# The hand-written order of the opening: the same steps in other places on the compute engines' queues

## The chip, the cores and the metric

One core of a Trainium2 chip. The metric is the device time of the kernel in microseconds, the median of several runs. One execution was also taken by the profiler; all times of single instructions come from that execution and are counted from the start of its span.

## The reference

A gated linear attention recurrence, whose output goes through a feed-forward block with a hard-swish gate. Everything is float32 (the weights come in as float64, as pairs of 32-bit words).

```python
# q, k, v, alpha: (batch 4, heads 8, seq 768, head_dim 48)
for t in range(S):
    state = alpha[:, :, t, :, None] * state + np.einsum('bhd,bhe->bhde', k[:, :, t], v[:, :, t])
    y[:, :, t] = np.einsum('bhd,bhde->bhe', q[:, :, t], state)
x = y.transpose(0, 2, 1, 3).reshape(B * S, H * D)       # 3072 x 384
h = x @ w_in                                            # 384 x 2048
g = h * np.clip(h + 3.0, 0.0, 6.0) / 6.0
out = g @ w_out                                         # 2048 x 384
```

## The kernel before

**Chunks and groups.** The 4 x 768 tokens are 24 chunks of 128 tokens (index `j`), six for each batch element. Two chunks make a group `g` of 256 tokens, for which the feed-forward block is computed. Groups 0 and 1 (chunks 0 to 3) take a plain path; from group 2 on, both matrix products go through sums and differences of blocks, with fewer multiplications (steps `M`, `n`, `o`, `e`, `h`; the second product does so from group 1 on, steps `s`, `P`, `K`, `G`). For that, sums of weight blocks have to be made first (`y` for `w_in`, `x` for `w_out`).

**The order.** Nothing is scheduled by the compiler. A string of words is run from first to last, and each word calls one step, which issues its instructions on one engine's queue. Each engine takes its own queue strictly in that order, and an instruction waits for its operands and buffers by semaphores. So the string sets five queues at once, and nothing else does. A word is a step's name and its numbers: `sc.1.0.2` is `scores(1, 0, 2)`.

**The steps of the opening**, by engine (line numbers are those of the profile):

- SP, loads: `la`, `lk`, `lq` (alpha, k, q of a chunk, L251; from chunk 6 on in blocks, L262), `lv` (v of a chunk in two halves, L272), `w.i` (one of 16 weight slices, L162, L166). A slice lands in one of five raw buffers, and a later slice reuses it.
- A weight slice is then made into float32 by `d1` (ACT, L186), `d2` (ACT, L196), `dx` (ACT, L191, slices 0, 1, 2, 4 only), `d3` (DVE, two instructions L203, L205 for those slices, three L207, L208, L210 for the others) and `d4` (POOL, L217), which needs all the others.
- Attention: `ta`, `tk`, `tq` transpose a chunk of alpha, k, q on PE (L282; from chunk 6 on DVE, L286). `ca` copies alpha (ACT, L300); `r` and `p` are scans over it (DVE, L309 and L320, `r` with a small reciprocal L313); `k` and `q` scale the transposed k and q (DVE, L332). `kb` transposes k back (PE, L374), `ck` copies it (ACT, L378). `u` is the state's update (PE, L429), `sm.j.0` and `sm.j.1` add it to the state (DVE, L437, L439), `st` decays the state (POOL, L409). `sc` computes scores (PE, L346), `m` masks them (DVE, L356, four instructions). `sv` and `qa` (ACT, L419, L366) put the state and q beside v and the scores; `sv.0.0` is a memset on POOL (L415). `ya`, `yb` give the chunk's output (PE, L455), `cy` copies it to `xT` (ACT, L464).
- Feed-forward of groups 0 and 1: `fa.i`, `fb.i` (PE, L489: one block of the first product for chunk 0, then for chunk 1), `f.g.i.m` (PE, L478: the same for a whole group), `fr` (ACT, L494) and `fg` (DVE, L498) the gate; `b` (PE, L516) the second product of group 0.
- `z` are idle matmuls on the identity (PE, L532).

**Buffers that order steps.** PSUM has four banks for the attention, `banks[0..3]`, and four for the feed-forward, `bank_m[0..3]`; the last numbers of a word say which it uses (`kb.2.0`: bank 0; `sc.2.0.2`: banks 0 and 2; `f.1.0.2`: block pair 0 of group 1, in `bank_m[2]`). A step that writes a bank waits until the step that reads its former contents is through. So `u.1.3.1` writes banks 3 and 1, `sm.1.0` reads bank 3, and `ya.0.3` can then write it.

**The padding.** From chunk 6 on, chunks are loaded in blocks into the tiles `quads`, two sets of three. The 16 columns that a load leaves unwritten must hold ones. Before, `load_akq` set them itself on POOL (`nc.gpsimd.memset`, L257, 32 partitions x 64 elements, two per tile) with the first load into each tile, ahead of that load's DMAs.

Of the kernel before, what the change touches and what calls it, by code (L numbers as in the profile page):

```python
# [17 lines left out]
def kernel(  # L18
# [228 lines left out]

    def load_akq(name, j):
        src = rows({"a": alpha, "k": k, "q": q}[name], j)
        if j < FIRST:  # L250
            nc.sync.dma_start(out=ring[name, j % NR][:, :, 0:D],  # L251
                              in_=src.rearrange("h s d -> s h d"))
            return
        to = quads[name, j % NQ]
        if j < FIRST + NQ:
            for o in (BLK, 3 * BLK):
                nc.gpsimd.memset(to[o : o + BLK, :, V - 1, D - BLK : BLK], 1.0)  # L257
        to = to.rearrange("r p v d -> r p (v d)")
        t = src.rearrange("(p a) (u v) d -> a u p (v d)", a=2, v=V)
        for o in range(4):  # L260
            skip = BLK * (o % 2)
            nc.sync.dma_start(out=to[BLK * o : BLK * (o + 1), :, 0 : V * D - skip],  # L262
                              in_=t[o // 2, :, :, skip : V * D])
# [457 lines left out]
    def store2(g, i):  # L721
# [8 lines left out]
        "lq": lambda j: load_akq("q", j), "lv": load_v, "w": load_weight,  # L730
# [14 lines left out]
    def run(words):  # L745
        for word in words.split():
            name, *at = word.split(".")
            steps[name](*(int(x) for x in at))

    with tc.manual_schedule():  # L750
        run("""z.0.5 z.0.3 z.0.1 z.0.8 qa.0.0 w.0 d2.0 d3.0 la.0 ta.0.0 ca.0 r.0 lk.0 tk.0.1 k.0
               z.0.2 p.0 la.1 ta.1.2 lq.0 tq.0.3 ca.1 r.1 lk.1 lv.0.0 sv.0.0 d1.0 kb.0.0 ck.0 z.0.2
               u.0.2.1 sm.0.0 sv.0.1 q.0 qa.0.1 tk.1.0 k.1 p.1 z.0.2 sc.0.2.3 m.0 la.2 ta.2.0 ca.2
               dx.0 w.2 d2.2 kb.1.0 ck.1 lq.1 r.2 sm.0.1 st.1 tq.1.2 q.1 d3.2 z.0.3 d1.2 dx.2 lv.1.1
               u.1.3.1 sv.1.0 sm.1.0 p.2 sm.1.1 sc.1.0.2 m.1 ya.0.3 yb.0 cy.0 lq.2 w.1 d1.1 tq.2.1
               q.2 d4.2 lk.2 tk.2.3 k.2 fa.2.0 d4.0 st.2 sc.2.0.2 d2.1 d3.1 m.2 dx.1 d4.1 qa.1.1
               lk.3 la.3 ta.3.1 ca.3 la.4 fa.0.1 sv.1.1 w.3 r.3 ta.4.3 ca.4 r.4 tk.3.1 k.3 kb.2.0
               qa.1.0 d2.3 ya.1.2 yb.1 cy.1 fa.1.2 lq.3 ck.2 d1.3 p.3 d3.3 lv.2.2 u.2.3.2 sm.2.0
               d4.3 fb.2 tq.3.1 q.3 fb.1 qa.2.0 sm.2.1 sv.2.0 st.3 fr.0.2.0 fg.0.2 lk.4 tk.4.0
               sv.2.1 w.5 d2.5 k.4 d3.5 d1.5 qa.3.0 d4.5 qa.2.1 sc.3.1.3 m.3 w.6 d2.6 d1.6 d3.6 d4.6  # L760
               lv.3.0 lq.4 w.7 kb.3.2 fb.0 f.0.3.3 kb.4.0 ya.2.1 ck.3 u.3.3.2 sm.3.0 fr.0.3.1 fg.0.3
               fr.0.1.0 fg.0.1 qa.3.1 sv.3.0 sm.3.1 p.4 d2.7 sv.3.1 d1.7 d3.7 d4.7 f.0.5.0 fr.0.5.1
               fr.0.0.0 fg.0.5 fg.0.0 tq.4.3 ck.4 la.5 ta.5.2 f.0.6.3 ca.5 w.4 d2.4 ya.3.0 yb.3 cy.3
               fr.0.6.1 yb.2 cy.2 w.9 d2.9 q.4 qa.4.1 d1.4 d1.9 dx.4 la.6 w.8 d3.4 r.5 lk.5 w.10
               d3.9 p.5 ca.6 fg.0.6 d4.9 w.12 lq.5 lv.4.1 d2.8 d3.8 f.0.7.2 d1.8 st.4 d4.8 d4.4 w.11
               fr.0.7.0 fg.0.7 f.1.7.0 fr.1.7.1 fg.1.7 sc.4.0.2 m.4 f.1.1.1 fr.1.1.0 fg.1.1 f.1.3.3
               fr.1.3.1 d2.10 d1.10 tk.5.3 f.1.0.2 d2.12 d3.10 d4.10 w.13 fg.1.3 fr.1.0.0 fg.1.0 k.5
               d3.12 lq.6 f.1.6.0 f.1.2.1 u.4.1.0 sm.4.0 d1.12 d4.12 sv.4.0 qa.4.0 ya.4.2 fr.1.6.1
               fg.1.6 w.15 tq.5.3 fa.4.3 sv.4.1 d2.11 kb.5.1 d2.13 fr.1.2.0 f.1.4.2 fr.1.4.1 d1.11
               sm.4.1 q.5 r.6 d3.11 d3.13 fg.1.4 d4.11 lv.5.0 lk.6 tq.6 p.6 d2.15 d3.15 fg.1.2 d1.13  # L770
               d4.13 sc.5.0.3 yb.4 f.1.5.0 fr.1.5.1 fg.1.5 tk.6 m.5 b.1.0.2 fb.4 b.1.1 d1.15 d4.15
               st.5 y.5 w.14 la.7 lk.7 cy.4 d2.14 qa.5.1 ck.5 b.0.0.1 fr.0.4.0 d3.14 k.6 q.6 ca.7
               fg.0.4 d1.14 d4.14 x.0 y.1 y.10 b.0.1 y.0 y.2 u.5.2 P.1.0.0 K.1.0 qa.5.0 sv.5.0
               qa.6.1 P.1.1.3 b.0.2 b.1.2 kb.6.0 ya.5.3 y.6 s.1.0.0 sm.5.0 sv.5.1 G.1.0.0 tk.7
               s.1.1.1 s.1.2.3 x.1 yb.5 cy.5 b.1.3 sc.6.1.2 lv.6.2 ck.6 u.6.3.0 s.1.3.2 x.2 P.1.2
               b.0.3 K.1.1 y.7 s.1.4 s.1.5 y.11 y.3 r.7 xc.2.1 x.3 y.4 y.8 xc.2.3 k.7 xc.2.0 xc.2.4
               y.9 y.12 y.16 y.13 y.15 P.1.3.3 K.1.2 P.1.4 bo.1 P.1.5 xc.2.5 G.1.1.1 P.1.6 y.14 y.17
               y.19 xc.2.6 sm.6.0 G.1.2.2 y.20 M.2.0.2 lv.12.1 la.8 O.1.1 O.1.0 ca.8 y.18 y.21 y.23
               so.1 G.1.3.3 n.2.0.8 bo.0 lq.7 lv.7.0 O.1.2 m.6 xc.2.2 xc.2.10 xc.2.7 tq.7 r.8 p.7
               xc.2.8 sv.6.1 M.2.15.3 M.2.1 kb.7.3 n.2.1.9 M.2.16 M.2.2 n.2.2.10 M.2.7.0 n.2.7.11  # L780
               sm.6.1 xc.2.9 q.7 p.8 M.2.3 M.2.4 n.2.4.12 M.2.8 o.2.0.0 M.2.5 n.2.5.13 qa.7.0 sv.6.0
               st.7 lk.8 O.1.3 lq.8 lk.9 la.9 la.10 tk.8 tq.8 lq.10 lq.9 ya.6.1 yb.6 M.2.9 z.1.3
               M.2.18.1 o.2.1.0 e.2.1.1 M.2.10 cy.6 ck.7 sc.7.0.2 u.7.1.3 n.2.10.14 M.2.11 qa.7.1
               ca.9 la.11 y.22 M.2.6.2 h.2.1 q.8 m.7 e.2.0.0 h.2.0 n.2.11.15 qa.6.0 n.2.18.10 qa.8.1
               M.2.12 M.2.19 n.2.12.12 M.2.13 sm.7.0 sv.7.1 r.9 k.8 o.2.3.0 sv.7.0 ya.7.0 y.24
               o.2.5.0 n.2.13.12 o.2.2.0 yb.7 cy.7 sc.8.1.2 xc.3.1 o.2.2.1 e.2.2.1 xc.3.3 o.2.3.1
               M.2.14 xc.3.4 xc.3.0 xc.3.5 o.2.4.0 xc.3.7 xc.3.6 o.2.6.0 P.2.0.1 M.3.0.2 M.2.17
               h.2.2 o.2.6.1 e.2.3.0 h.2.3 o.2.7.0 K.2.0 n.3.0.12 M.3.1 n.3.1.9 e.2.5.1 M.3.7.0
               n.3.7.13 xc.3.8 o.2.7.1 xc.3.2 kt.8 e.2.6.0 h.2.6 tk.9 M.3.2 n.3.2.10 e.2.4.0 P.2.1.3
               h.2.4 h.2.5 s.2.0.14 e.2.7.0 G.2.0.1 h.2.7 M.3.3 M.3.4 n.3.4.8 k.9 s.2.1.11 M.3.8  # L790
               o.3.0.0 ca.10 kt.9 P.2.3.3 s.2.2.15 s.2.3.14 lv.8.2 kw.8 kr.8 lk.10 sm.7.1 xc.3.9
               M.3.5 n.3.5.11 K.2.2 e.3.0.1 xc.3.10 M.3.9 o.3.1.0 P.2.2 K.2.1 u.8.0.3 M.3.18.2 s.2.5
               M.3.10 n.3.10.14 n.3.18.15 e.3.1.0 s.2.4 P.2.4 tq.9 h.3.0 st.8 sv.8.0 M.3.11 n.3.11.8
               tk.10 p.9 sm.8.0 q.9 r.10 k.10 qa.9.0 qa.9.1 m.8 sm.8.1 h.3.1 M.3.19 o.3.5.0 kt.10
               P.2.5 G.2.2.0 st.9 M.3.12 sc.9.0.1 qa.8.0 n.3.12.10 o.3.3.0 kw.9 lv.9.0 kr.9 sv.8.1
# [137 lines left out]
```

## Time and profile before

| | |
|---|---|
| median of 3 runs | 534.24 us (534.19 to 534.98) |
| profiled execution, its own time | 533.84 us |
| its span, first to last instruction | 531.80 us |
| PE busy | 522.2 us (98%) |
| PE weight loads busy | 496.9 us (93%) |
| DVE busy | 477.0 us (90%) |
| ACT busy | 257.4 us (48%) |
| POOL busy | 50.4 us (9%) |
| HBM read, written | 44.50 MB, 8.91 MB |
| granted TensorE clock, mean | 1.0 |

A row of the timeline has the start in us, the duration in us, engine, line, operation, output and inputs, shapes and the number of instructions merged; in brackets the idle time of the engine before it and what ended it. Busy times of PE run to the modelled end of a matmul, which is later than the start of the next one. PEld is the loading of weights into PE, which runs beside the matmuls.

### The profile page before, as it was taken

To read this page: it belongs to the slowest core of one execution; us is meant where nothing else is said; L and a number is where in the kernel's file an instruction comes from. 1 tells how busy PE (TensorE), PEld (TensorE's weight loads), DVE (VectorE), ACT (ScalarE), POOL (GpSimd) and SP (SyncE) were. 2 spreads that over 40 slices of the span, in tenths; PEclk is the share of its full clock that TensorE was granted. 3 is DMA by queue.
4 is the path that set the end of the run, shared out by engine and by line. 5 is a ranking of instruction groups with operands and counts; after the bars stand their busy time and mean duration, and the time that the engine had idled before them with its cause. 6 is when DMAs were issued, how large, how long until landed. Compare 5 with 4: busy or idle time off the path is not lost.

```text
span 531.8 us, 15143 instructions
## 1 busy us (share of the span) xinstructions
PE 522.2 (98%) x6306; PEld 496.9 (93%) x6306; DVE 477.0 (90%) x849; ACT 257.4 (48%) x503; POOL 50.4 (9%) x71
## 2 busy tenths in 40 slices
PE   7799999999999999999999999999999999999997
PEld 7698886789999999999999999999999999999997
DVE  6999989999999999999999999999999899496382
ACT  3889865212653553553544444642634544553340
POOL 5333425100000000000000000000000000000000
PEclk9999999999999999999999999999999999999999
DMA  9998887006615156254345356055364052100001
GB/s 173 218 254 247 211 231 156 18 2 149 155 31 118 30 125 139 49 137 100 89 107 118 90 123 143 18 134 111 92 138 105 10 110 44 44 2 2 15 16 37
DMA packets 124100, 54.40 MB, mean 102 GB/s; under 512 B 83328, under 2 KB 116864, under 8 KB 124032
## 3 DMA queue, kind: packets, MB, share of 16 engines
q1 hardware_dynamic: 124032, 53.44, 44.0%
q8 instruction: 49, 0.80, 0.7%
q14 instruction: 19, 0.16, 0.1%
HBM read 44.50 MB, written 8.91 MB: 100 GB/s over the span
## 4 chain that ended last, share of the span: by engine, by line
PE 81%; DVE 9%; ACT 3%; DMA 3%; POOL 2%; issue 1%; SPq 0%; DVEq 0%; POOLq 0%; ACTq 0%
PE m_ps L703 34%; PE m_ps L600 34%; PE m_ps L478 4%; PE t_ps L455 3%; PE t_ps L346 2%; PE t_ps L429 2%; DMA v<-in_v_dram 1%; DMA raw<-in_moe_w_out_dram 1%; DVE rings L647 1%; DVE R L309 1%; DVE raw L537 1%; ACT raw L186 1%; DVE g_sb L647 1%; ACT raw L191 1%; DVE w L537 1%
## 5 line engine op out<-in xcount | busy, mean ns | idle before, releaser
L606 ACT COPY g_sb<-m_ps 128x512 f32<-128x512 f32 x110 | 63.6, 584 | 123.7 <-PE m_ps L600 104.3
L703 PE MATMUL m_ps<-w,g_sb 128*128 128x192 f32 x704 | 121.7, 327 | 0.0
L703 PEld LDWEIGHTS m_ps<-w,g_sb 128*128 128x128 f32 x704 | 113.7, 190 | 0.4
L703 PE MATMUL m_ps<-rings,g_sb 128*128 128x192 f32 x528 | 91.5, 326 | 0.0
L703 PEld LDWEIGHTS m_ps<-rings,g_sb 128*128 128x128 f32 x528 | 85.4, 190 | 0.1
L600 PE MATMUL m_ps<-xc,w 128*128 128x128 f32 x640 | 82.8, 277 | 0.4 <-DVE w L541 0.4
L600 PEld LDWEIGHTS m_ps<-xc,w 128*128 128x128 f32 x640 | 77.5, 192 | 1.7 <-issue 0.6
L494 ACT ACTIVATE r<-g_sb,half 128x512 f32<-128x512 f32 x80 | 56.8, 722 | 33.1 <-DVE g_sb L541 12.1
L498 DVE SCALAR_TENSOR_TENSOR g_sb<-r,g_sb 128x512 f32<-128x512 f32 x80 | 53.7, 683 | 4.3 <-ACT r L494 3.9
L600 PE MATMUL m_ps<-xT,raw 128*128 128x128 f32 x400 | 52.5, 277 | 0.0
L600 PEld LDWEIGHTS m_ps<-xT,raw 128*128 128x128 f32 x400 | 48.6, 192 | 0.6
L409 POOL TENSOR_TENSOR st<-sm,R 128x192 f32<-128x192 f32 x20 | 12.9, 643 | 352.2 <-DVE sm L439 305.5
L647 DVE TENSOR_TENSOR g_sb<-g_sb 128x512 f32<-128x512 f32 (+1 forms) x55 | 41.9, 792 | 0.2
L600 PE MATMUL m_ps<-xT,w 128*128 128x128 f32 x320 | 42.0, 276 | 0.0
L600 PEld LDWEIGHTS m_ps<-xT,w 128*128 128x128 f32 x320 | 39.3, 192 | 0.1
L366 ACT COPY A<-q 48x256 f32<-48x256 f32 x88 | 35.6, 404 | 5.0 <-DVE q L332 3.8
L356 DVE TENSOR_TENSOR A<-t_ps,mask 64x256 f32<-64x256 f32 x96 | 36.0, 413 | 0.4
L478 PE MATMUL m_ps<-xT,w 128*128 128x256 f32 x144 | 32.8, 382 | 0.1
L600 PE MATMUL m_ps<-xc,raw 128*128 128x128 f32 x240 | 31.8, 276 | 0.0
L309 DVE TENSOR_TENSOR_SCAN R<-t,ones 128x516 f32<-128x516 f32 x24 | 29.6, 1235 | 1.0 <-ACT t L300 0.9
L478 PEld LDWEIGHTS m_ps<-xT,w 128*128 128x128 f32 x144 | 26.7, 190 | 3.8 <-POOL w L217 0.2
L600 PEld LDWEIGHTS m_ps<-xc,raw 128*128 128x128 f32 x240 | 29.6, 192 | 0.1
(104 smaller groups left out, 725.8 us busy)
## 6 DMA issues: line engine op xcount, KB each, us to landing
raw<-in_moe_w_out_dram SPq DMA_DIRECT2D x8, 768.0 KB, 5.3
raw<-in_moe_w_in_dram SPq DMA_DIRECT2D x6, 768.0 KB, 6.6
v<-in_v_dram SPq DMA_DIRECT2D x48, 96.0 KB, 3.1
out_dram<-oh SPq DMA_DIRECT2D x44, 96.0 KB, 1.7
far<-kq SPq DMA_DIRECT2D x64, 64.0 KB, 2.2
kb<-far SPq DMA_DIRECT2D x64, 64.0 KB, 2.1
aq<-in_alpha_dram SPq DMA_DIRECT2D x36, 96.0 KB, 2.7
qq<-in_q_dram SPq DMA_DIRECT2D x36, 96.0 KB, 2.5
```

Of the source, the lines that this page charges most:

```text
L309: nc.vector.tensor_tensor_scan(out=reverse(R, n - 1, n), data0=reverse(ax, n, n), data1=reverse(ones, n, n), initial=0.0, op0=ALU.mult, op ...
L356: nc.vector.tensor_tensor(out=to[:, a], in0=sc[a][half], in1=mask[half, half].unsqueeze(1).to_broadcast([HB, NP, HB]), op=ALU.mult)
L366: nc.scalar.copy(out=to[:, a], in_=Q_t[j][64 * a : 64 * a + D, :, half])
L409: nc.gpsimd.tensor_tensor(out=st, in0=sm, in1=R_t[j][:, :, 0:1].to_broadcast([C, NP, D]), op=ALU.mult)
L455: nc.tensor.matmul(y_of(j, (i + 1) // 2, p)[:, HB * b : HB * b + HB], vb[:, p, e : e + 32], A_t[j][:, b, 2 * p + a], start=(b == 0 and i = ...
L478: nc.tensor.matmul(h[:, f], w1[:, kk, o : o + C], xT_t[g][:, kk], start=(kk == 0), stop=(kk == KT - 1))
L494: nc.scalar.activation(out=to, in_=h, func=AF.Relu, bias=half, scale=1.0 / 6.0)
L498: nc.vector.scalar_tensor_tensor(out=to, in0=r, scalar=1.0, in1=h, op0=ALU.min, op1=ALU.mult)
L600: nc.tensor.matmul(acc[g][i][:, f * C : (f + 1) * C], spots[w][:, f * C : (f + 1) * C], x_of(g, x), start=(first and f == 0), stop=last, s ...
L606: nc.scalar.copy(out=slots[z], in_=acc[g][i])
L647: nc.vector.tensor_tensor(out=out, in0=in0, in1=in1, op=ALU.subtract)
L703: nc.tensor.matmul(to[g], a, rhs[:, f], start=(first and f == 0), stop=(last and f == HF - 1), skip_group_check=True)
```

## The change

The words up to the first quarter of the string stand in another order; from `lk.8` on (1355 words) it is unchanged. Of the 433 words ahead of that, the same are there, and two new ones, `pd.0` and `pd.1`. The order of the SP words, which are all loads and stores, is the same. On PE, DVE, ACT and POOL, steps change places. The padding memsets leave `load_akq` and become a step of their own, `pd`, one word for each of the two sets of tiles (six memsets each).

```diff
+    def pad(r):
+        for name in "akq":
+            for o in (BLK, 3 * BLK):
+                nc.gpsimd.memset(quads[name, r][o : o + BLK, :, V - 1, D - BLK : BLK], 1.0)
+
     def load_akq(name, j):
...
         to = quads[name, j % NQ]
-        if j < FIRST + NQ:
-            for o in (BLK, 3 * BLK):
-                nc.gpsimd.memset(to[o : o + BLK, :, V - 1, D - BLK : BLK], 1.0)
...
-        run("""z.0.5 z.0.3 z.0.1 z.0.8 qa.0.0 w.0 d2.0 d3.0 la.0 ta.0.0 ca.0 r.0 lk.0 tk.0.1 k.0
-               z.0.2 p.0 la.1 ta.1.2 lq.0 tq.0.3 ca.1 r.1 lk.1 lv.0.0 sv.0.0 d1.0 kb.0.0 ck.0 z.0.2
-               u.0.2.1 sm.0.0 sv.0.1 q.0 qa.0.1 tk.1.0 k.1 p.1 z.0.2 sc.0.2.3 m.0 la.2 ta.2.0 ca.2
...
+        run("""z.0.5 z.0.3 z.0.1 qa.0.0 w.0 d2.0 d3.0 la.0 ta.0.0 z.0.8 lk.0 tk.0.1 la.1 ta.1.2
+               lq.0 tq.0.3 lk.1 lv.0.0 d1.0 ca.0 r.0 p.0 k.0 kb.0.0 z.0.2 z.0.2 q.0 la.2 dx.0 ca.1
+               r.1 ck.0 u.0.2.1 sm.0.0 qa.0.1 sv.0.1 tk.1.0 p.1 sc.0.2.3 w.2 lq.1 sm.0.1 k.1 m.0
...
```

The queues that result, engine by engine, at the places of which the prediction speaks (`-` before, `+` after):

```diff
-PE:   z.0.5 z.0.3 z.0.1 z.0.8 ta.0 tk.0 z.0.2 ta.1 tq.0 kb.0 z.0.2 u.0 tk.1 z.0.2 sc.0 ta.2 kb.1 tq.1 z.0.3
-      u.1 sc.1 ya.0 yb.0 tq.2 tk.2 fa.2 sc.2 ta.3 fa.0 ta.4 tk.3 kb.2 ya.1 yb.1 fa.1 u.2 fb.2 tq.3 fb.1 tk.4
-      sc.3 kb.3 fb.0 f.0.3 kb.4 ya.2 u.3 f.0.5 tq.4 ta.5 f.0.6 ya.3 yb.3 yb.2 f.0.7 f.1.7 sc.4 f.1.1 f.1.3
-      tk.5 f.1.0 f.1.6 f.1.2 u.4 ya.4 tq.5 fa.4 kb.5 f.1.4 sc.5 yb.4 f.1.5 b.1.0 fb.4 b.1.1 b.0.0 b.0.1 ...
+PE:   z.0.5 z.0.3 z.0.1 ta.0 z.0.8 tk.0 ta.1 tq.0 kb.0 z.0.2 z.0.2 u.0 tk.1 sc.0 ta.2 z.0.2 kb.1 tq.1 u.1
+      z.0.3 ya.0 yb.0 sc.1 fa.0 tq.2 tk.2 fa.2 sc.2 ta.3 ta.4 kb.2 ya.1 yb.1 tk.3 fa.1 fb.2 fb.1 tq.3 u.2 tk.4
+      fb.0 sc.3 kb.3 kb.4 f.0.3 ya.2 yb.2 u.3 f.0.5 tq.4 f.0.6 ta.5 ya.3 yb.3 f.0.7 f.1.1 f.1.7 sc.4 f.1.3
+      f.1.0 f.1.6 f.1.2 u.4 tk.5 fa.4 f.1.4 kb.5 tq.5 b.0.0 ya.4 yb.4 sc.5 u.5 b.0.1 f.1.5 fb.4 b.1.0 b.1.1 ...
-DVE:  d3.0 r.0 k.0 p.0 r.1 sm.0.0 q.0 k.1 p.1 m.0 r.2 sm.0.1 q.1 d3.2 sm.1.0 p.2 sm.1.1 m.1 q.2 k.2 d3.1 m.2 ...
+DVE:  d3.0 r.0 p.0 k.0 q.0 r.1 sm.0.0 p.1 sm.0.1 k.1 m.0 r.2 q.1 sm.1.0 p.2 d3.2 sm.1.1 m.1 q.2 k.2 d3.1 m.2 ...
-DVE:  ... p.6 d3.15 fg.1.2 fg.1.5 tk.6 m.5 y.5 d3.14 k.6 q.6 ca.7 fg.0.4 x.0 ...
+DVE:  ... p.6 d3.13 tk.6 m.5 fg.1.4 d3.15 d3.14 fg.1.5 sm.5.0 fg.0.4 ca.7 tk.7 s.1.0.0 x.0 k.6 ...
-ACT:  d2.0 ca.0 ca.1 d1.0 ck.0 sv.0.1 qa.0.1 ca.2 dx.0 d2.2 ck.1 d1.2 dx.2 sv.1.0 cy.0 d1.1 d2.1 dx.1 ...
+ACT:  d2.0 d1.0 ca.0 dx.0 ca.1 ck.0 qa.0.1 sv.0.1 d1.2 ca.2 d2.2 ck.1 dx.2 sv.1.1 cy.0 qa.1.1 sv.1.0 d1.1 d2.1 dx.1 ...
-POOL: sv.0.0 st.1 d4.2 d4.0 st.2 d4.1 d4.3 st.3 d4.5 d4.6 d4.7 (la.6: pads) d4.9 st.4 d4.8 d4.4 d4.10 (lq.6: pads) ...
+POOL: d4.0 pd.0 sv.0.0 pd.1 st.1 d4.2 st.2 d4.1 d4.3 st.3 d4.5 d4.6 d4.7 d4.9 st.4 d4.8 d4.4 d4.10 d4.12 d4.11 ...
```

## The prediction

> **What bounds the kernel now.** The table by stretches says where time can be won at all. Its columns: stretch and length, busy time (and instructions) of PE, PEld, DVE, ACT and POOL, granted clock, DMA share and GB/s.
>
> ```profile
> core 0: us, PE busy (x) PEld busy (x) DVE busy (x) ACT busy (x) POOL busy (x), PEclk, DMA share, GB/s
> 0.00:20.00 20.00, 15.45 (x152) 13.61 (x152) 14.99 (x30) 10.00 (x15) 7.12 (x20) 1.00 1.16 204
> 20.00:32.00 12.00, 10.30 (x273) 9.03 (x274) 11.81 (x21) 11.63 (x17) 6.91 (x5) 1.00 1.01 202
> 32.00:52.00 20.00, 20.00 (x332) 17.91 (x332) 19.59 (x33) 18.42 (x35) 6.12 (x5) 1.00 0.93 251
> 52.00:128.00 76.00, 75.50 (x661) 61.67 (x650) 73.78 (x114) 35.30 (x62) 19.11 (x25) 1.00 0.50 126
> ```
>
> From 32 us on PE is never idle except 0.5 us before 128 us, and nothing is reordered after 128 us. PE does the same matmuls in both kernels (the idle ones of its `z` steps too). So the change is worth what PE stands still before 32 us, plus that 0.5 us, against any new standstill. The timeline of PE names the stops; a record runs 0.16 us past its successor's start, so a real stop is about 0.16 longer than the bracket.
>
> ```profile
> 1.47 6.67 PE L532 MATMUL m_ps<-ident 128*128 128x128 f32 x34 [1.47 <-POOL ident masks.py:199]
> ...
> 20.03 0.69 PE L429 MATMUL t_ps<-v,kb 64*48 64x48 f32 x32 [0.95 <-issue]
> 20.55 0.69 PE L346 MATMUL t_ps<-q,k 48*64 48x64 f32 x32
> 22.16 1.10 PE L455 MATMUL t_ps<-A,v 128*32 128x64 f32 x64 [0.92 <-DVE s L439]
> 23.55 1.16 PE L282 MATMUL t_ps<-ident,rings 128*128 128x128 f32 x8 [0.29 <-DVE sm L439]
> 24.94 1.60 PE L489 MATMUL m_ps<-xT,w 128*128 128x128 f32 x12 [0.24 <-POOL w L217]
> ...
> 30.64 1.30 PE L455 MATMUL t_ps<-A,v 128*32 128x64 f32 x64 [0.23 <-ACT A L366]
> ...
> 127.89 1.13 PE L600 MATMUL m_ps<-xc,w 128*128 128x128 f32 x8 [0.42 <-DVE w L541]
> ```
>
> The first row holds idle matmuls: 34 in 6.50 us (the next row starts at 7.97), where six of them later take 0.67, so some 26 ran at half rate, until about 7.0 us. The 20.03 row is `u.1`: it waits for the second half of `lv.1`, issued at 13.0 us, and the DMA view has 7.0 us to landing for it:
>
> ```profile
> v<-in_v_dram SPq DMA_DIRECT2D x2, 96.0 KB, 7.0
> ```
>
> The DMA share is above 1 up to there and SP issues the same loads in the same order, so `u.1` starts at about 20.05 in the new kernel too, if its other inputs are ready. All that PE wins or loses earlier is swallowed there.
>
> **Part 1: up to `u.1`.** (a) `z.0.8` moves behind `ta.0`. PE's first 18 records end near 5.5 us, it idles until `la.0` lands at 6.9 (issued 1.25, 5.7 us to landing), and `ta.0` runs at 7.0 instead of 8.0. (b) ACT does `d1.0` (0.82) ahead of `ca.0` and `dx.0` (1.7 to 1.95) behind it; `ca.0` ends at 8.2 (8.6 to 9.2 before), and `r.0` follows `d3.0` on DVE at 8.25 instead of 9.22. (c) `p.0` (1.14) goes ahead of `k.0`, so `kb.0` comes at 11.6 instead of 11.4; `u.0` waits for `lv.0` until 13.3 either way. (d) POOL now does `d4.0` (1.86) after `dx.0`, about 10.9 to 12.7, not at 24.86. The scan `r.1` falls into it; the 29.45 scan took 1.62 instead of 1.23 beside a `d4`, so I charge 0.6. (e) `ta.2` needs the bank that `k.1` reads, and `k.1` now ends at 16.45 (15.5 before); `ca.2` stands behind `d1.2`, whose `w.2` lands at 16.2, and ends at 17.75; then `kb.1` 0.6, `ck.1` 0.5 behind `d2.2`: ready at 19.0. Bound: nothing wins before 20.05; with a late clock (rival B) it is 20.0. Taken: 0, covered by `lv.1`, with up to 1.0 us to spare.
>
> **Part 2: `u.1` to `fa.1`.** Two orders matter. `z.0.3` (0.67) goes behind `u.1`, where it is no longer free: +0.67. And on DVE `sm.1.0` and `p.2` now precede `d3.2`. Before, it was the reverse:
>
> ```profile
> 20.41 0.71 DVE L203 TENSOR_SCALAR w<-w 128x768 f32<-128x768 f32 x1
> 21.15 0.69 DVE L205 TENSOR_SCALAR w<-w 128x768 uint32<-128x768 uint32 x1
> 21.76 0.34 DVE L439 TENSOR_TENSOR s<-t_ps,st 128x192 f32<-128x192 f32 x1
> ```
>
> `d3.2` held `sm.1.0` until 21.76, and `ya.0` needs its bank: that is the 0.92 stop. Now `sm.1.0` runs at 20.8, when `u.1` is done, and `z.0.3` covers PE until 21.25. DVE itself now waits some 0.9 us (from `q.1`'s end, 19.85, to 20.8), since `d3.2` is queued behind `sm.1.0`. Its chain from there, start to start: `sm.1.0` 0.27, `p.2` 1.14, `d3.2` 1.35, `sm.1.1` 0.27, `m.1` 1.55, `q.2`, `k.2` 0.6 each, `d3.1` 1.35 (1.75 before, when `d4.0` ran beside it), then three of `m.2`'s four operations 1.15: bank 0 is free at 29.1.
>
> PE: 20.05 + `u.1` 0.52 + `z` 0.67 + `ya.0`,`yb.0` 1.1 + `sc.1` 0.62 + `fa.0` 1.4 (drawn forward: `d4.0` is long done, `cy.0` ends at 23.1) + `tq.2`,`tk.2` 0.9 + `fa.2` 1.45 (`d4.2`, 23.65 to 25.5, is just in time) + `sc.2` 0.62 + `ta.3`,`ta.4` 0.94 = 28.3. `kb.2` then waits until 29.1, the one stop left. + `kb.2` 0.49, `ya.1`,`yb.1` 1.1, `tk.3` 0.5, `fa.1` 1.5 = 32.7. Before, the same steps ended at 33.41. PE leads by **0.7** (0.5 to 0.95, as the switches between forms cost 0 or 0.14 each).
>
> **Part 3: 33 to 128 us.** PE runs without stops if each producer keeps its place. The tight places: `ya.2` needs three operations of `m.3` (DVE 41.2, bank free at 42.35; PE there 42.6); `f.0.7` needs `d4.7` (50.6; PE 51.6), which drops the 0.15 us stop at 52.27; `f.1.0` needs `fg.0.7`, which stands on DVE behind `d3.8`, and `fr.0.7`, on ACT behind `d1.9 d1.4 dx.4 d2.8 qa.4.0 d1.8` (5.9 us): 62.4 against PE's 62.9. `r.6` and `q.4` are earlier, `k.5`, `p.5` later, at equal sums. The padding memsets (12 of 0.14 us) leave the places before `la.6`, `lq.6`, `lk.6` for 13 to 15 us, where POOL waits anyway; `st.1` still follows `sm.0.1` closely, and no matmul hears of it before `sm.1.0`.
>
> DVE gains more than PE, because two `d4` no longer fall on operations with which they collide:
>
> ```profile
> 81.73 2.02 POOL L217 TENSOR_TENSOR w<-raw 128x768 int32<-128x768 int32 x1 [0.17 <-POOL kq L257]
> 82.40 1.77 DVE L207 TENSOR_SCALAR w<-w 128x768 f32<-128x768 f32 x1
> 92.69 1.96 DVE L332 TENSOR_TENSOR q<-q,P 128x512 f32<-128x512 f32 x1
> ```
>
> Undisturbed these two DVE operations take 0.56 and 0.69: 2.5 us lost. In the new order `d4.13` runs beside `tk.6` and `m.5`, and `d4.14`, `d4.15` beside `fg.1.5`, `sm.5.0`, `fg.0.4`, `ca.7`, `tk.7`, like the pairs that show no stretch (`m.3` beside the 41.58 `d4`). So DVE ends its weight sums (`y.23`, 127.74 before) at about 125.3, while PE asks at 126.6: the 127.89 stop goes, 0.42 by its bracket, 0.58 start to start; I take 0.45.
>
> **Sum.** -0.7 - 0.15 - 0.45 = **-1.3 us** (ends: -2.0 if `kb.2`'s stop vanishes too; 0 if the tight places give the lead back). The profiled execution took 533.84, 2.04 around its span of 531.80; 533.84 - 1.3 = 532.5. The median of the runs is 534.24, 0.40 above it, so I predict **532.9**. A change of 0.2% (1.07 us) is about the least that a measurement of this kernel can tell from none.
>
> **Rivals.** *A. The lead is given back (0.24).* The DVE order costs 0.9 us of waiting at 20 us, and DVE is over 97% busy from 20 to 128. If `d3.2`, `m.1` or `m.3` come 0.7 us later than I sum, `kb.2`, `ya.2` and `f.1.0` wait and only the last stop remains as gain: 534.24 - 0.45 = 533.8 (533.2 to 534.3). For it: slacks of 0.25 and 0.5 us. Against: the same DVE work stood before `m.3` in both kernels.
>
> *B. The matmul clock opens late (0.10, slower).* In the new order PE idles 1.5 us just before the moment (7.0) at which it got its full rate. The first row had half rate for 5.5 us from its first matmul; counted again from `ta.0` that is until 12.5. Then `z.0.8` takes 3.4 instead of 1.8 us, `tk.0` ends at 12.1, `ck.1` at 20.0 and `q.1` at 21.05: a price of 0.3, and no slack left. If the rate stays at half until after 20 us, the chain `k.1`, `ta.2`, `ca.2`, `kb.1` makes `u.1` start near 22.2, 2.1 late, with some 1.3 more at half rate behind it: 532.9 + 3.4 = 536.3. Past 21.35 for `u.1` it is slower than before. Against it: from 7.0 on PE works without a break for some 5 us.
>
> The Trainium skill (TensorE: Matmul & The Clock Gate, Part 1) says that the full rate comes after one window of about 3.4 us of sustained work. By that rule it comes at some 10.4 us, `ck.1` is ready at 19.5, the price is 0 instead of 0.3, and B would have half its chance; no trace here shows an interrupted start.
>
> *C. A new stop on the way (0.16).* `f.1.0` at 62.9: if `w.8` or ACT's six steps ahead of `fr.0.7` come 2 us later than summed, PE stops 1.5 us there and three bank reuses behind it (`f.1.6`, `f.1.2`, `b.1.0`) have too little slack to give it back; with one more such stop, 3 us: 534.4 to 536, middle 535.4. For it: ACT was 98% busy in 40 to 50. Against: its share falls to under half after 52. Beyond a loss of 1.3 us the result is slower than before.
>
> **Numbers.** Forecast 0.50 (532.0 to 533.2). Faster by over 0.2% is its 0.50; within it A and 0.03 of C, 0.27; slower the rest of C and B, 0.23. The range 532.0 to 535.4 leaves out the upper half of C, B, and gains over 2.2 us.
>
> **What would show it.** Right: `u.1` at 20.0 again; `sm.1.0` before 21.2; one stop before `kb.2` near 29; no PE stop from 32 to 128, none at `M.2.1`; no DVE `L207` or `L332` above 1.2 us at 80 to 95; PE's first steady row (`L600` after 125 us) about 1 us earlier, and all later rows shifted equally. Wrong: `u.1` past 21 us, idle matmuls at 0.2 us beyond 11 us, or a bracket above 0.3 us between 33 and 128.

## The result and the profile after

The changed kernel took **531.71 us** (median of 6 runs, 531.33 to 532.26) against 534.22 for the kernel before in the same comparison: ratio 0.9958, 95% interval 0.9946 to 0.9969. Measured again (E1) it was 531.73 against 533.59, ratio 0.9962 (0.9949 to 0.9974). Forecast was 532.9 with a range down to 532.0: faster, as said, but the time lies below the range. The kernel before came out at 533.64 as the median of 97 runs in the five later comparisons (533.49 to 533.83 in each), so the 534.24 of the first three runs was high, and the change is worth some 1.9 us, not 2.5.

The profiled execution of the changed kernel took 531.87 us, with a span of 530.1 (before: 533.84 and 531.80). The same table by stretches (stretch, length, busy time of PE, PEld, DVE, ACT, POOL, clock, DMA share, GB/s):

```profile
core 0: us, PE busy (x) PEld busy (x) DVE busy (x) ACT busy (x) POOL busy (x), PEclk, DMA share, GB/s
0.00:20.00 20.00, 13.88 (x154) 12.22 (x158) 15.71 (x30) 11.39 (x16) 11.65 (x34) 1.00 1.14 195
20.00:32.00 12.00, 11.73 (x285) 10.44 (x286) 11.10 (x21) 10.99 (x20) 4.19 (x3) 1.00 1.05 217
32.00:52.00 20.00, 19.71 (x328) 17.49 (x327) 19.08 (x32) 17.88 (x32) 6.38 (x5) 1.00 0.92 250
52.00:128.00 76.00, 76.00 (x659) 62.77 (x658) 74.04 (x121) 35.17 (x61) 15.98 (x11) 1.00 0.52 135
```

PE is busy for 11.73 us of the stretch from 20 to 32, where it was 10.30, and for all of 52 to 128. DVE's busy time from 20 to 32 falls from 11.81 to 11.10. The timeline of PE, with its remaining stops:

```profile
1.46 4.18 PE L534 MATMUL m_ps<-ident 128*128 128x128 f32 x18 [1.46 <-POOL ident masks.py:199]
6.96 0.63 PE L284 MATMUL t_ps<-ident,rings 128*128 128x128 f32 x4 [1.31 <-DMA rings<-in_alpha_dram]
...
19.43 0.26 PE L431 MATMUL t_ps<-v,kb 64*48 64x48 f32 x2 [0.29 <-issue]
19.91 0.57 PE L431 MATMUL t_ps<-v,kb 64*48 64x48 f32 x30 [0.22 <-DMA v<-in_v_dram]
20.41 0.94 PE L534 MATMUL m_ps<-ident 128*128 128x128 f32 x6
21.27 1.10 PE L457 MATMUL t_ps<-A,v 128*32 128x64 f32 x64
...
28.97 0.66 PE L376 MATMUL t_ps<-ident,k 128*128 128x128 f32 x4 [0.27 <-DVE A L358]
...
42.66 1.10 PE L457 MATMUL t_ps<-A,v 128*32 128x64 f32 x64 [0.29 <-DVE A L358]
...
126.24 1.10 PE L602 MATMUL m_ps<-xc,w 128*128 128x128 f32 x8
```

`u.1` begins at 19.43 and waits for `lv.1` after two matmuls (19.91), `ya.0` follows at 21.27 without a stop (22.16 before), one stop stands before `kb.2` at 28.97 (forecast 29.1), a small one that was not forecast before `ya.2` at 42.66 (the 19.71 us of the third row above), and none at `M.2.1`. DVE at the place of the swap:

```profile
20.59 0.36 DVE L441 TENSOR_TENSOR s<-t_ps,st 128x192 f32<-128x192 f32 x1 [0.38 <-PE t_ps L431]
20.86 1.22 DVE L322 TENSOR_TENSOR_SCAN P<-t 128x516 f32<-128x516 f32 x1
22.00 0.66 DVE L203 TENSOR_SCALAR w<-w 128x768 f32<-128x768 f32 x1
```

The starts of the same PE steps in the profiled executions show where the time went. The first column of times is the third matmul of `u.1`, the first that needs the late half of `lv.1`; the last is the lead over the first profile of before at `M.2.0`. The profile of E3 alone has a stop of 0.63 us at 34.98, put down to "issue", which the table's lead of -0.14 contains.

| | `u.1` | `kb.2` | `fa.1` | `ya.2` | `f.0.7` | `M.2.0` | lead |
|---|---|---|---|---|---|---|---|
| before | 20.16 | 29.81 | 31.87 | 43.30 | 52.27 | 125.52 | |
| after | 19.91 | 28.97 | 31.08 | 42.66 | 51.48 | 124.46 | 1.06 |
| after again (E1) | 20.21 | 29.27 | 31.38 | 42.95 | 51.77 | 124.75 | 0.77 |
| early order only (E2) | 19.56 | 28.63 | 30.74 | 42.30 | 51.12 | 125.11 | 0.41 |
| late order only (E3) | 20.00 | 29.64 | 31.70 | 43.86 | 52.68 | 125.66 | -0.14 |
| E5 | 19.48 | 30.23 | 32.34 | 43.66 | 52.48 | 125.46 | 0.06 |
| E15 | 19.94 | 28.91 | 31.03 | 42.67 | 51.49 | 124.47 | 1.05 |
| E16 | 19.61 | 30.34 | 32.45 | 43.79 | 52.61 | 125.59 | -0.07 |

Behind `M.2.0`, the start of `M.2.1` moves from 127.89 to 126.24, and the lead goes from 1.06 to 1.65; the end of the span comes 1.70 earlier.

### The profile page after: what moved, and what is told of

Its sections match the earlier page's. It is cut to its first block, busy times and chain, and to the rows that moved or that the text cites. A ratio compares the mean times of both kernels' runs of the same rounds, so it can differ in the third digit from the quotient of the medians.

```text
span 530.1 us, 15131 instructions
## 1 busy us (share of the span) xinstructions
PE 520.6 (98%) x6306; PEld 495.8 (94%) x6306; DVE 474.8 (90%) x849; ACT 257.5 (49%) x503; POOL 49.9 (9%) x71
## 4 chain that ended last, share of the span: by engine, by line
PE 92%; DMA 2%; DVE 2%; ACT 2%; POOL 0%; issue 0%; SPq 0%
PE m_ps L705 38%; PE m_ps L602 35%; PE m_ps L480 5%; PE t_ps L457 4%; PE m_ps L518 4%; PE t_ps L348 2%; PE t_ps L431 2%; DMA v<-in_v_dram 1%; DMA rings<-in_alpha_dram 1%; ACT raw L191 1%; DVE R L311 1%; PE m_ps L491 1%; PE t_ps L284 0%; POOL w L217 0%; PE m_ps L534 0%
```

## Experiments

T is the theory that was tested each time, R its rival. "Before" is 533.59 for E1 to E4, 533.49 for E5 to E8, 533.67 for E9 to E12, 533.83 for E13 and E14, 533.74 for E15 and E16.

**E1, the changed kernel again.**

> The changed kernel once more. The profiled executions differ by 1.97 us (span -1.70, around the span -0.27), the medians by 2.51. Theory T (the traces are typical, the profiled execution of before was only a short one): the difference of medians comes out at -2.0 to -2.6 again, and a second profile has the same stops in the opening (z.0.8 behind ta.0, u.1 at 19.9, kb.2 29.0, ya.2 42.7, M.2.1 without a stop) and a span of 529.5 to 530.2. Rival R (the first comparison was a lucky draw): -1.3 to -1.9, as the prediction summed.

531.73 us, 1.86 below before. That is R's range (-1.3 to -1.9) and not T's (-2.0 to -2.6): the first comparison made the change look larger than it is. The other half of T holds: all the stops are there again, 0.3 us later, and so was the landing of `lv.1` (20.16 instead of 19.86). The distance from `u.1`'s third matmul to `M.2.0` is 104.55 in the first profile and 104.54 here: what differs between these two executions happens ahead of it.

**E2 and E3, the halves.** The first 192 words (to some 51 us, the same set of steps in both, and the two `pd` in E2) in one order, the rest up to `M.2.0` in the other.

```diff
 E2:  first 192 words of the changed string and its 2 pd, then the words of the old string
 E3:  first 192 words of the old string, then the words of the changed string (memsets in load_akq)
```

> The new order for the first 192 steps (to about 51 us, the same set of steps in both kernels), then the old order from there to M.2.0. T: PE comes to this point 0.8 us earlier, but DVE comes to it 0.7 us later than in the kernel before (52.41 against 51.72), and the old order behind it is the one in which DVE sets M.2.1. So PE's lead is lost there and the stop at M.2.1 grows from 0.58 to 1.5 or more: 0 to +0.7 us against before. Rival R, the prediction's sum (lead 0.7 and the 0.15 stop are won by themselves): -0.8 to -1.2.

> The old order for the first 192 steps, then the new one. T: PE starts without the lead, DVE 0.7 us ahead of where it is in the changed kernel, so the stop at M.2.1 is gone (0.58), and the fewer changes of matmul form between 52 and 124 us are worth 0.27: -0.8 to -1.1 us against before. Rival R, the prediction's sum (last stop only): -0.45. If E2 and E3 add up to the whole change, the halves are independent; T has them not add up, since the new late order is what makes room for a later DVE.

E2: 533.36, ratio 0.9992 (0.9984 to 1.0001), 0.2 us. E3: 532.72, ratio 0.9982 (0.9973 to 0.9991), 0.9 us. Together 1.1 of the 1.9 us: the halves do not add up, as T said. E3 is in T's range; E2's 0.2 us gained lies just outside T's (0 to 0.7 lost) and far from R's. The place in E2 was another than T's:

```profile
60.45 1.78 PE L480 MATMUL m_ps<-xT,w 128*128 128x256 f32 x7 [0.47 <-DVE g_sb L500]
...
127.50 1.13 PE L602 MATMUL m_ps<-xc,w 128*128 128x128 f32 x8 [0.44 <-DVE w L543]
```

PE reaches `f.0.7` 1.15 us earlier than before. Of this 0.5 us is there at the end of `u.1`: `lv.1` landed early, at 19.52, and in the new order `u.1` was ready for it (in the old one it would not have been, as the account of Part 1 below shows). Then `f.1.0` at 60.45 waits for `fg.0.7`, which stands on DVE behind `d3.8`: the tight place of the prediction's rivals A and C. The stop at `M.2.1` did not grow, it merely stayed. In E3 neither is there:

```profile
126.55 1.06 PE L600 MATMUL m_ps<-xT,raw 128*128 128x128 f32 x8
127.44 1.10 PE L600 MATMUL m_ps<-xc,w 128*128 128x128 f32 x8
```

and from `f.0.7` to `M.2.0` it takes 72.98 us, exactly as the changed kernel does, where before took 73.25 without any stop in it. In the old order PE enters the small matmuls (`sc`, `u`, `ya`, `yb`: 48 or 64 rows, or 32 columns) six times in this stretch, in the new one five times; by the starts around such an entry (`L516` to `L429` 0.09 us longer than a steady step, `L429` to `L703` 0.12, the next one 0.10) one costs 0.3 us. That the 0.27 lies in the later order is shown; that it is this entry is read from the starts.

**E4, `z.0.3` back ahead of `u.1`.**

```diff
-... dx.2 lv.1.1 u.1.3.1 z.0.3 lq.2 ...
+... dx.2 lv.1.1 z.0.3 u.1.3.1 lq.2 ...
```

> The changed kernel with the idle step z.0.3 back ahead of u.1. T: kb.2 and ya.2 wait for DVE, whose chain begins at sm.1.0 right behind u.1, so the 0.67 that z.0.3 costs behind u.1 was hidden: a stop of 0.3 opens at ya.0, the one at kb.2 grows to 0.6, and the time stays (-0.1 to +0.1 against the changed kernel, -2.5 against before). Rival R, the prediction's term (+0.67 of a place on the path): 0.3 to 0.67 faster than the changed kernel.

531.63, ratio 0.9959 (0.9945 to 0.9973): the changed kernel's time. A stop of 0.52 opens at `ya.0` (21.08), and `kb.2` still comes at 29.05. The 0.67 that the prediction charged for `z.0.3` behind `u.1` is on no path; from `u.1` to `M.2.0` it is 104.28 instead of 104.54, which is all that it can be worth. It is the fastest of the versions run, by less than can be told from the changed kernel.

**E5 and E7, the swap on DVE undone in the new order, and done alone in the old one.**

```diff
 E5, changed string:
-sm.1.0 p.2 d3.2 sm.1.1 ...
+d3.2 sm.1.0 p.2 sm.1.1 ...
 E7, old string:
-q.1 d3.2 z.0.3 d1.2 dx.2 lv.1.1 u.1.3.1 sv.1.0 sm.1.0 p.2 sm.1.1 ...
+q.1 z.0.3 d1.2 dx.2 lv.1.1 u.1.3.1 sv.1.0 sm.1.0 p.2 d3.2 sm.1.1 ...
```

> The changed kernel with d3.2 back ahead of sm.1.0 and p.2 on DVE (the reverse of the swap that the prediction's Part 2 is built on). T: q.1 ends at 20.2, d3.2 takes until 21.55, so ya.0 starts at 21.9 instead of 21.3; but DVE no longer waits 0.4 us for u.1 and its chain is as much earlier, so kb.2 comes at 29.3 instead of 29.0 and the stop at ya.2 goes: 0 to +0.3 us against the changed kernel (-1.6 to -1.9 against before by the 21 runs). Rival R (the prediction's reason: the swap removes a stop of 0.92): +0.6 to +0.9 against the changed kernel.

> The kernel before with one edit: d3.2 behind sm.1.0 and p.2. T: the stop of 0.92 at ya.0 goes (ya.0 at 21.2), but d3.2 now ends at 23.45, sm.1.1 runs at 23.5 instead of 23.16 and d4.2 ends at 25.4, so that tq.2 and fa.2 wait for them: +0.2 to +0.6 us against before. Rival R, the prediction's reason taken by itself: -0.5 to -0.9.

E5: 532.69, ratio 0.998 (0.9971 to 0.9989), 1.0 us slower than the changed kernel. R's number, T's failed; but the trace shows something that neither had:

```profile
21.58 0.34 DVE L441 TENSOR_TENSOR s<-t_ps,st 128x192 f32<-128x192 f32 x1
21.80 1.86 POOL L217 TENSOR_TENSOR w<-w,raw 128x768 int32<-128x768 int32 x1 [5.03 <-DVE w L205]
21.84 2.91 DVE L322 TENSOR_TENSOR_SCAN P<-t 128x516 f32<-128x516 f32 x1
```

The earlier `d3.2` frees `d4.2` on POOL 0.04 us ahead of the scan `p.2`, and the scan takes 2.91 us instead of 1.22. E7: 534.43, ratio 1.0021 (1.0012 to 1.003), 0.9 us *slower* than before. The 0.92 stop at `ya.0` is gone (21.16), as the prediction's Part 2 said; in its place:

```profile
23.86 1.77 PE L282 MATMUL t_ps<-ident,rings 128*128 128x128 f32 x8 [1.61 <-DVE sm L439]
25.60 2.51 PE L489 MATMUL m_ps<-xT,w 128*128 128x128 f32 x12
```

`tq.2` waits 1.61 for `sm.1.1`, now behind `d3.2`: T's direction, at twice its size. That `fa.2` is drawn out to 2.51 is not POOL's doing (`d4.2`, 1.86 us from 23.68, was through at 25.54). Behind the stop the granted clock fell, and until 27.47 the matmuls are 0.213 us apart, then 0.112; the column after POOL is the clock:

```profile
20.00:24.00 4.00, 2.36 (x129) 2.03 (x129) 3.54 (x7) 3.88 (x6) 0.70 (x2) 1.00 1.22 252
24.00:28.00 4.00, 4.00 (x20) 3.56 (x19) 3.92 (x8) 3.99 (x5) 4.00 (x3) 0.57 0.98 197
```

This profiled execution took 534.97. The loss does not depend on the clock: the seven of E7's eleven executions with a mean clock of 0.999 or 1.0 took 534.30 to 534.49, still 0.9 above the like ones of before (533.48).

**E15 and E16, the stop and the meeting parted.** E13 was meant for this and failed: with `p.2` behind `m.1`, `m.1` had to wait 1.44 us for `sc.1` (which in the new order stands behind `ya.0`), and `p.2` met `st.2` on POOL.

```diff
 E13:  d3.2 sm.1.0 sm.1.1 ya.0.3 yb.0 sc.1.0.2 m.1 p.2 d4.2 ...
 E15:  sm.1.0 d3.2 p.2 sm.1.1 ya.0.3 yb.0 sc.1.0.2 m.1 d4.2 ...
 E16:  sm.1.0 d3.2 sm.1.1 p.2 ya.0.3 yb.0 sc.1.0.2 m.1 d4.2 ...
```

> E5 again (the changed kernel with d3.2 ahead of sm.1.0), but with p.2 moved behind sm.1.1 and m.1, so that the scan no longer starts together with d4.2 on POOL. In E5 the scan took 2.91 instead of 1.22 us, and the kernel lost 1.0 us against the changed one. T2: the loss of E5 is this meeting; the later ya.0 (21.95) by itself costs little, since kb.2 waits for DVE: m.2 is done 0.4 us earlier than in the changed kernel and PE comes to kb.2 at 29.2: -0.2 to +0.3 us against the changed kernel. Rival R (the loss of E5 is the stop of 1.07 us at ya.0, as the prediction's Part 2 had it): +0.7 to +1.0.

E13: 533.66, ratio 0.9998 (0.9988 to 1.0007), 1.9 us slower than the changed kernel. Inconclusive, for the wait named.

> The changed kernel with d3.2 drawn forward between sm.1.0 and p.2 on DVE (sm.1.0, d3.2, p.2, sm.1.1, m.1). sm.1.0 stays at 20.6, so ya.0 has no stop; p.2 stands directly behind d3.2 and starts, as DVE's rows are spaced, 0.2 us before d4.2 can start on POOL. T2 (an operation that has begun is not held by a POOL sum): p.2 takes 1.22 us, m.1 starts at 23.6 as in the changed kernel, kb.2 at 29.0: -0.2 to +0.2 us against the changed kernel. If a scan is held wherever it overlaps a POOL sum: p.2 takes some 2.7 us and the kernel loses about 1 us.

> E15 with sm.1.1 ahead of p.2 (sm.1.0, d3.2, sm.1.1, p.2, m.1): the scan p.2 now starts just behind the start of d4.2 on POOL, and there is still no stop at ya.0. T2: p.2 is held until 0.13 us before d4.2 ends and takes 2.7 to 2.9 us, m.1 starts 1.5 us later than in the changed kernel, kb.2 with it: +0.9 to +1.6 us against the changed kernel, without any stop at ya.0. Rival R (the loss of E5 was the stop at ya.0): -0.2 to +0.2.

E15: 531.84, ratio 0.9958 (0.9944 to 0.9971), the changed kernel's time. E16, with two neighbours exchanged: 533.01, ratio 0.999 (0.9981 to 0.9999), 1.2 us slower. First E15, then E16:

```profile
22.22 1.22 DVE L322 TENSOR_TENSOR_SCAN P<-t 128x516 f32<-128x516 f32 x1
22.43 2.65 POOL L217 TENSOR_TENSOR w<-w,raw 128x768 int32<-128x768 int32 x1 [6.26 <-DVE w L205]
```

```profile
21.98 0.34 DVE L441 TENSOR_TENSOR sm<-t_ps,s 128x192 f32<-128x192 f32 x1
22.19 1.84 POOL L217 TENSOR_TENSOR w<-w,raw 128x768 int32<-128x768 int32 x1 [5.30 <-ACT v L421]
22.23 2.89 DVE L322 TENSOR_TENSOR_SCAN P<-t 128x516 f32<-128x516 f32 x1
...
27.93 0.69 PE L348 MATMUL t_ps<-q,k 48*64 48x64 f32 x32 [1.43 <-DVE k L334]
```

Whoever starts first keeps the other out: in E15 the scan runs its 1.22 and the sum is drawn out to 2.65, which nobody waits for; in E16 the scan is held, and PE stops for 1.43 at `sc.2`. `ya.0` has no stop in either. So the 1.0 us of E5 was the meeting; the stop of 1.07 that E5 also had at `ya.0` cost nothing beside it, because `kb.2` waits for DVE's chain: from `u.1`'s third matmul to `M.2.0` E5 with the stop and E16 without it both take 105.98. In the changed kernel, the DVE order is worth that `p.2` runs while POOL is idle.

**E6 and E8, the two terms that were put at nothing.** E6: `z.0.8` back ahead of `ta.0`. E8: the memsets back in `load_akq`.

> The changed kernel with the idle step z.0.8 back ahead of ta.0. T: ta.0 comes at 8.0 instead of 7.0 and with it ca.0 and r.0 (9.2 instead of 8.2); of this some 0.2 to 0.5 us reach sm.1.0 and kb.2, since DVE runs almost without a stop from r.0 to q.1. Rival R, the prediction's term: nothing, since u.1 waits for lv.1 anyway. To be read from the times of r.0, q.1, u.1, sm.1.0 and kb.2 in the trace; one execution cannot tell 0.3 us in the total.

> The changed kernel with the padding memsets back in the load steps (12 of them ahead of la.6, lq.6, lk.6, la.7, ... on POOL instead of two steps at 13 us). T and the prediction agree: no matmul hears of it, the same stops on PE at the same times within 0.1 us once the landing of lv.1 is taken off. A rival: the loads behind them are held back and the late d4 come later, which would show as a stop of PE between 52 and 128 us or at M.2.1.

One execution each, 532.09 and 532.35. In E6 `r.0` starts at 9.51 instead of 8.24 and `u.1` at 20.15; `lv.1` landed at 18.92 there and covered nothing, so this is the chain's own time, and `M.2.0` is 0.23 later than in the first profile of after. The 0 of Part 1 holds where `lv.1` lands at 20 and is a few tenths where it lands earlier. In E8 `lv.1` landed at 20.42, and from `u.1` to `M.2.0` it is 104.52: the pads cost nothing.

**E9 and E10, 1.14 us more for DVE.** The scan `p.6` a second time on DVE, at 108.5 and 107.4 us.

```diff
 E9, old string:       ... s.1.3.2 x.2 +p.6 P.1.2 ...
 E10, changed string:  ... q.6 bo.1 +p.6 K.1.0 ...
```

> The kernel before with the scan p.6 done a second time on DVE at about 110 us (1.14 us start to start; no POOL sum runs there, nothing uses its result). It measures how far DVE is from being the bound ahead of M.2.1. T: before, DVE sets M.2.1 (stop of 0.58), so all of it shows: +1.0 to +1.2 us.

> The changed kernel with the same second scan p.6 at about 105 us. T: in the new order DVE stands 0.5 us for PE at 115.8 and its last weight sum ends 0.45 us before PE asks for it at M.2.1, so some 0.9 to 1.0 of the 1.14 us is covered: 0 to +0.3 us against the changed kernel. Rival R (DVE is still the bound, the changed kernel has only moved it): +0.8 to +1.1.

E9: 535.10, ratio 1.0023 (1.0015 to 1.0032), 1.4 us slower than before and above T's 1.0 to 1.2. E10: 531.86, ratio 0.9967 (0.9955 to 0.9979), 0.1 us slower than the changed kernel. `M.2.1` in E9 and in E10:

```profile
129.33 1.13 PE L600 MATMUL m_ps<-xc,w 128*128 128x128 f32 x8 [1.01 <-DVE w L541]
```

```profile
126.01 1.13 PE L602 MATMUL m_ps<-xc,w 128*128 128x128 f32 x8
```

Before, every microsecond of DVE ahead of `M.2.1` was one of the kernel; after, DVE has about one to spare. In E9's profile `f.0.7` to `M.2.1` takes 76.79 us (from 52.54) instead of 75.62, which is 1.17 for a scan of 1.14; the other 0.27 lies ahead of `f.0.7`, where `u.2` waited for `lv.2` (33.90).

**E11 and E12, which moves the swap needs.** E7 with `d4.0` right behind `dx.0`, and that with `fa.0` ahead of `tq.2`.

```diff
 E11:  ... ca.2 dx.0 +d4.0 w.2 d2.2 ...  (and taken out behind fa.2.0)
 E12:  E11, and ... lq.2 w.1 d1.1 +fa.0.1 tq.2.1 ...  (taken out behind la.4)
```

> The kernel before with the swap of E7 (d3.2 behind sm.1.0 and p.2) and d4.0 drawn forward on POOL, right behind dx.0. T: d4.2 then ends at 25.5 instead of 27.4 (in E7 d4.0 ran ahead of the end of the pair), fa.2 starts whole, and d3.1 no longer meets d4.0 (0.76 us of DVE in E7); the stop of 1.6 us at tq.2 stays: +0.1 to +0.5 us against before, 0.4 to 0.8 less than E7. Rival R (the swap wins its 0.92 as soon as POOL is free): -0.5 to -0.9.

> E11 with fa.0 drawn forward on PE ahead of tq.2. T: 1.45 us of matmuls fill most of the stop at tq.2 (fa.0 can start when cy.0 ends, about 23.9), kb.2 comes at 29.3 instead of 29.8: -0.1 to -0.6 us against before; the stop at M.2.1 stays, since DVE has not become faster behind 33 us. So the swap, d4.0 and fa.0 pay only together. Rival R (fa.0 only changes places with the later work): the same as E11.

E11: 535.61, ratio 1.0039 (1.0027 to 1.0051), 1.9 us slower than before; E12: 534.60, ratio 1.0023 (1.0013 to 1.0033), 0.9 us slower. Both theories missed E11, and T missed E12 (0.1 to 0.6 faster than before):

```profile
20.84 0.51 POOL L409 TENSOR_TENSOR st<-sm,R 128x192 f32<-128x192 f32 x1
...
21.39 0.36 DVE L439 TENSOR_TENSOR s<-t_ps,st 128x192 f32<-128x192 f32 x1 [0.96 <-POOL st L409]
```

In the old ACT order `dx.0` ends at 18.8, so `d4.0` occupies POOL from 18.9 to 20.9, `st.1` waits behind it and `sm.1.0` behind that. In the changed kernel `dx.0` stands ahead of `ca.1` on ACT, `d4.0` is done at 12.6 and `st.1` runs at 15.7.

The clock takes part as well. First E11, then E12:

```profile
24.00:28.00 4.00, 3.50 (x16) 3.32 (x17) 3.92 (x10) 3.99 (x5) 2.33 (x2) 0.57 0.97 234
```

```profile
24.00:28.00 4.00, 3.79 (x36) 3.70 (x38) 3.73 (x9) 3.96 (x6) 2.33 (x2) 1.00 0.98 176
```

Six of E11's seven executions had a mean clock of 0.996 or 0.997; the seventh, at 0.999, took 534.52. Eight of E12's twelve had 1.0 and took 534.11 to 534.62. `fa.0` shortens the stop (1.61 before `tq.2` in E11, 1.19 before `fa.0` in E12), but at an equal clock nothing won by it shows, as E12's R had it. The 1.0 us between E11 and E12 is mostly that the clock stayed at full rate more often. At full clock E7, E11 and E12 all lose some 0.9. That the swap pays only with `dx.0` and `d4.0` early, which Part 1 of the prediction counted at nothing, is read from E11's wait for `st.1`; the old order with both drawn forward was not run.

**E14, the kernel before, a second profile.**

> The kernel before, unchanged, for a second profile. T: a span of 531.2 to 531.8 with the same stops, and about 1.8 us around the span as in all other runs (2.04 in the first profile was a single high value); a time of 533.2 to 533.8. Rival: the first profile is typical, 2.04 around the span, and a time of 534.2.

534.18 us with a span of 532.4. The 1.8 around the span is T's, the time R's: `lv.1` landed at 20.79, and `u.1`'s third matmul ran at 20.92 instead of 20.16. The granted clock was 0.57 from 21 to 25 us, but from that matmul to `M.2.0` it is 105.18, no more than the 105.36 of the first profile. In all profiles but the first of before, 1.73 to 1.86 us lie around the span.

## Why the prediction was off

The forecast had the places right at which PE would win its time. The base of the sum was wrong, and so were one wait and two sizes.

- **The base.** "The median of the runs is 534.24, 0.40 above it, so I predict 532.9." That step failed: three runs made the base, and it was 0.6 us above what 97 later runs gave. From 533.64 the same sum would have given 532.3, 0.6 above the result.
- **Part 1: 0, "covered by `lv.1`".** 0.14 was won: the step behind `u.1` starts at 20.41 instead of 20.55. That it was so little is luck, since the reason was misread. The prediction has `u.1` before as waiting for "the second half of `lv.1`"; it waited for `ck.1`, which stood behind `dx.0` and `d2.2` on ACT. First before, then after:

```profile
16.86 1.93 ACT L191 ACTIVATE raw<-raw 128x768 f16<-128x768 int32 x1
18.53 0.93 ACT L196 ACTIVATE w<-raw 128x768 f32<-128x768 f32 x1
19.35 0.58 ACT L378 COPY kb<-t_ps 128x512 f32<-128x512 f32 x1
```

```profile
18.75 0.58 ACT L380 COPY kb<-t_ps 128x512 f32<-128x512 f32 x1
```

  `ck.1` ended at 19.93 and `u.1` began at 20.03; the load, landed at 20.02, was just in time. In E3, with the same early order, it landed at 19.35, and `u.1` still began at 19.87, 0.10 behind `ck.1`. In the new order `ck.1` ends at 19.33 and `u.1` begins at 19.43: there it is the load that decides, and where it lands early, 0.5 us is won (E2). The prediction had "ready at 19.0", so of the "up to 1.0 us to spare" 0.5 was there.
- **Part 2: 0.7.** 0.79 at the start of `fa.1`, 0.65 once the 0.14 of Part 1 is taken off. `sm.1.0` at 20.59 (20.8), `ya.0` at 21.27 (21.25), `kb.2` at 28.97 (29.1). The size was right; of the reasons given, DVE's chain to `m.2` decided. "that is the 0.92 stop" and the +0.67 for `z.0.3` describe PE ahead of a step that waits for DVE anyway (E4, E5, E16), and the swap alone loses (E7).
- **Part 3, `ya.2`.** "bank free at 42.35; PE there 42.6" failed: the bank was free at 42.6, since DVE waits 0.36 for `ca.3` ahead of `r.3` (29.61), which the sum did not have, and PE was there at 42.2. The 0.15 lost there came back at `f.0.7`, where the 52.27 stop went as forecast; so Part 3's 0.15 did not come on top of Part 2, and the lead at `f.0.7` is 0.79 again.
- **33 to 125 us: nothing was charged for PE's own order.** 0.27 was won, since the new order enters the small matmuls once less (E3). The prediction priced such switches (0 or 0.14) in Part 2 only.
- **`M.2.1`: 0.45.** 0.59 was won. The prediction had 0.58 start to start and took less. The reason stands: from 78 to 96 us no `L207` takes more than 0.56 us and no `L334` more than 0.67, DVE's last weight sum ends 0.45 us before PE asks, and E9 against E10 shows DVE no longer sets the end.

The steps above make 0.79 + 0.27 + 0.59 = 1.65, and the span ends 1.70 earlier, for a sum of 1.3; with 0.6 from the base that is 1.0 of the 1.2 us missed. The last 0.2 is within the interval of the comparison. Of the rivals, A is what E2 shows: without the new later order the lead is given back at `f.1.0`. C did not happen in the changed kernel. B happened in part, without a price (below).

## What to carry to other kernels

A stop that is read from PE is worth only what the next wait behind it leaves: follow the engine that this wait names (here DVE at `kb.2`) before crediting the stop. When an operation is moved on DVE, look at which POOL operation it sets free and what will start beside it: exchanging two neighbours moved the kernel by 1.2 us. When a step could have waited for two things that end 0.1 us apart, find an execution in which one of them came early (here E3) before calling the other covered. And take a forecast's base from many runs, since the landing of one early load moved the profiles of the changed kernel by 0.55 us (after against E8) and a closed clock goes with slower executions (next section).

## What the runs showed of the hardware

**DVE and POOL shut each other out.** A held DVE operation is not slowed in proportion; it begins when POOL's ends. Taking its undisturbed duration from its end gives its true start:

| kernel | POOL operation ends | DVE operation, start + took - alone | earlier by |
|---|---|---|---|
| before | 81.73 + 2.02 = 83.75 | `L207`: 82.40 + 1.77 - 0.56 = 83.61 | 0.14 |
| E5 | 21.80 + 1.86 = 23.66 | `L322`: 21.84 + 2.91 - 1.22 = 23.53 | 0.13 |
| E16 | 22.19 + 1.84 = 24.03 | `L322`: 22.23 + 2.89 - 1.22 = 23.90 | 0.13 |
| E13 | 25.57 + 0.52 = 26.09 | `L322`: 25.60 + 1.57 - 1.22 = 25.95 | 0.14 |

So the price of a meeting is what is left of the POOL operation less 0.13 us. Masks and state updates, which read PSUM beside one SBUF tile, ran beside `d4.2` at their usual time in the kernel before (`L439` at 23.16 in 0.33 us, the four `L356` from 23.40 in 1.52). The Trainium skill (SBUF — State Buffer, "Who interferes with whom") calls it an exclusive lock: whichever starts first has the shared ports for its whole instruction and the other fully blocks, and of DVE's operations it names those with two SBUF inputs or in a two-port mode. The traces agree, for a scan too, and in both directions (E15's sum of 2.65).

**The matmul clock after a break.** In both traces the first matmuls run 0.21 us apart, twice the later 0.11 (the column of the granted clock reads 1.00 there all the same). In the first profile of after, the 16 of `z.0.8` behind the break at 5.6 to 7.0 us run 0.11 apart; in E1, E5 and E13, which have the same break, they are slow until 10.2 to 10.7, and in E16 the clock opened at 4.4, closed again at 8.0 and reopened near 11:

```profile
8.00:12.00 4.00, 4.00 (x24) 4.00 (x23) 3.35 (x5) 2.11 (x2) 1.80 (x1) 0.59 1.48 163
```

The column after POOL is the granted clock, 0.59 of full speed. This is rival B's beginning; `u.1` began at 19.47 to 19.70 in these four, 19.43 in the first profile of after, so its price ahead of `u.1` was 0.3 us at most. By the Trainium skill (TensorE: Matmul & The Clock Gate, Part 1) the window of about 3.4 us is free-running and the same kernel sees the change at different matmuls; the spread of these runs agrees. Counted from `ta.0`, the full rate came after 3.2 us in E1 and E5 and after 3.7 in E13.

The clock also closed later, behind stops on PE: in E7 and E11 behind the 1.61 at `tq.2`, in E14 behind stops of 1.00 and 0.52 ahead of `u.1`, each time to 0.50 for some 3.3 us. Of the 97 executions of the kernel before, 26 had a mean clock of 0.997, and their median is 534.03 against 533.57 for the rest; of 28 executions of the changed order and of its variants that take its time (after, E1, E4, E6, E8, E10, E15) one had. What of those 0.46 us is the clock is open, as E14 shows no loss by `M.2.0`, and no run shows why the same kernel closes it in one execution and not in another.

**One load sets the execution.** The second half of `lv.1`, issued at about 13 us, landed between 18.8 and 20.8 us in these profiles. In four with the changed order behind `u.1`, or nearly it (after, E1, E8, E15), `M.2.0` follows `u.1`'s third matmul by 104.52 to 104.55 us: nearly all that differs between these profiles is this landing. In the old order it shows only where it comes later than `ck.1`, as in E14.
